# A retention and low-rank mixer kernel: batch 0's q loaded one head at a time, and a planner that counts on more loads in flight

## The chip, the core and the metric

The kernel runs on one core of one Trainium2 chip. A core has five engines that run side by side: TensorE (PE in the profile; matrix products, with weight loads shown as PEld), VectorE (DVE), ScalarE (ACT), GpSimd (POOL) and SyncE (SP, which here only issues DMAs). Each follows its own list of instructions in order, and waits for the others through semaphores. Sixteen DMA engines move data between the memory (HBM) and the on-chip memory SBUF. Products go into PSUM, which has eight banks.

The metric is the time of one execution on the device, in microseconds (us). Less is better.

## The reference

Inputs are q, k and v of shape (4 batches, 8 heads, 768 steps, 64), a pair of low-rank matrices U (768 x 32) and V (32 x 768), and the weights of two layers, w_ch1 (512 x 2048) and w_ch2 (2048 x 512), all float32. First comes a retention (an attention with a decay for each head):

```
gamma = 1 - 2 ** (-5 - arange(H)); scale = 1 / sqrt(D)
for t in range(S):
    state = gamma * state + outer(k[:, :, t], v[:, :, t])
    y[:, :, t] = scale * (q[:, :, t] @ state)
```

The heads are laid side by side to x (4, 768, 512), and then

```
h = x.transpose(0, 2, 1) @ U @ V
u = x + h.transpose(0, 2, 1)
out = u + maximum(u @ w_ch1, 0) @ w_ch2
```

## The kernel before

**Stages.** The four batches go through the same stages: load q, k and v; scale and cast them to bf16; transpose k and q; scores, masked by time order; states that carry earlier blocks; a mix that gives x; the low-rank product (`proj`, `expand`, in batch 0 `low0` and `high0`) that gives u; a transpose of u (tile uT); the first layer ("up" products M<-w1b,uT, with a relu into gT) and the second (products of gT, or of its sums S, with w2b or its sums T). The second layer uses a scheme that trades eight products of blocks for seven and some sums on VectorE and GpSimd (tiles S and T). While TensorE does one batch's layers, the next batch's attention is put between them. Batches 0 and 1 go by pairs of heads (`pair`, c = 0 to 3); batches 2 and 3 by blocks of 128 steps (`chunk`).

**Loads.** The profile gives all plain loads of q, k, v, U and V the line L342, since they go through one helper, `load`. In batch 0 the list `ORDER` says "k0 q0 q1 k1 v0 k2 q2 q3 k3 v1 v2 v3": each name is one load of a tensor's head pair, 384 KB, into one of nine buffers `in`. `load_pair` makes them. k0 and v3 come in two loads of one head each, the others in one load. A q load has 256 rows of 1536 bytes (128 partitions times two heads), a k or v load has 768 rows of 512 bytes. All loads of batch 0 write a common key "in", and so keep their order in SP's list. The loads of batch 1 and 2 onward are made by `load_pair` and `loads_chunk` (three loads of 1024 rows for each block). Weights come by GpSimd's own queue (`load_cast`, L357), which casts to bf16 on the way. In batch 1 the transposes of k (kT<-kb, L542) and in batches 2 and 3 those of k and q (L717) and of u (uT<-x, L841) are DMAs too, issued by SP in the same queue as the loads.

**Casts.** In `pair`, the casts of q are two, one for each head (`cast`, qb<-in, L299 on GpSimd or L297 on ScalarE). The planner may give either to either engine in batch 0. The transposes of q (six TensorE instructions of L309) wait for both; ScalarE then copies the result (qT<-M).

**The planner.** The order of the work isn't written out. Every piece of work is a step with a cost on each engine that could do it, a due time `at`, an earliest time `hold`, and what it reads and writes. `Plan.run` runs a model of the core at build time: at each turn it takes the step that could start first, and among equals the one with the earlier due time. The sequence so found, with the engine chosen for each step, is the program. The planner's times are not in the program; only the order, and the choice of engines, are. For steps of SP (loads and DMA transposes) the model has two limits, in `when`: at most 8 DMAs of SP in flight, and at most 2350 rows (`op.dma[0]`) in flight together; a step that would go over is modelled as starting later, and another may then go first.

**Dummies.** Up to a planned 27 us, `fill` puts products of zeros (M<-gT, 128x512) into TensorE's planned gaps, so that it stays active. Their number follows from the planned gaps.

Of the kernel before, what the change touches and what calls it, by code (L numbers as in the profile page):

```python
# [65 lines left out]
class Plan:  # L66
# [11 lines left out]
    def add(s, cost, fn, rd=(), wr=(), at=0.0, mode=None, lock="", dma=None,  # L78
            hold=0.0, slack=0.0):
        op = Step(len(s.steps), cost, fn, at, mode, lock, dma, hold, slack)  # L80
        op.rd, op.wr = list(rd), list(wr)
        before = set()
        for r in rd:
            if r in s.writer:
                before.add(s.writer[r])
        for w in wr:
            before.update(s.readers.get(w, ()))
            if w in s.writer:
                before.add(s.writer[w])
        for r in rd:  # L90
            s.readers.setdefault(r, []).append(op)
        for w in wr:
            s.writer[w] = op
            s.readers[w] = []
        before.discard(op)
        for p in before:
            p.after.append(op)
        op.left = len(before)
        s.steps.append(op)
        return op  # L100
# [16 lines left out]
    def run(s, fill=None, until=0.0, traced=None, behind=None):  # L117
        free = {e: 2.03 if e == "A" else 0.85 for e in s.OVER}
        lock = {"D": 0.0, "P": 0.0}
        todo = {e: [] for e in s.OVER}  # L120
        mode, queues, flying, order = None, Queues(), [], []

        def offer(op):
            for e in op.cost:
                todo[e].append(op)

        def when(op, e):
            t = max(free["P" if e == "Q" else e], op.ready(e))
            if e in op.lock:
                t = max(t, lock["D" if e == "P" else "P"])  # L130
            if e == "S":
                fly = sorted((o.end, o.dma[0]) for o in flying if o.end > t)
                if len(fly) >= 8:
                    t = max(t, fly[-8][0])
                while fly and sum(n for _, n in fly) + op.dma[0] > 2350:
                    t = max(t, fly.pop(0)[0] - 1.2)
            return t

        for op in s.steps:
            if not op.left:  # L140
                offer(op)
        while len(order) < len(s.steps):
            best = None
            for e, ops in todo.items():
                for op in ops:
                    t = when(op, e)
                    turn = op.mode and op.mode[0] != mode
                    key = (t, op.at + (0.3 if turn else 0.0), op.n)
                    if best is None or key < best[0]:
                        best = (key, e, op)  # L150
            (t0, _, _), e, op = best
            for e2 in op.cost:
                todo[e2].remove(op)
            order.append(op)
            d = op.cost[e]
            op.start, op.eng = t0, e
            if op.dma:
                nd, lead = op.dma[0], op.dma[2]
                if e == "S":
                    flying = [o for o in flying if o.end > t0] + [op]  # L160
                free["P" if e == "Q" else e] = op.free = t0 + d
                queues.put(e, t0 + d + lead, op)
            else:
                if e == "PE":
                    if mode is not None and op.mode[0] != mode:
                        d += s.SWITCH
                    mode = op.mode[1]
                free[e] = op.free = t0 + d - s.OVER[e]
                op.end = t0 + d
                if e in op.lock:  # L170
                    lock[e] = op.end
            for n in op.after:
                n.pre.append(op)
                n.left -= 1
                if not n.left:
                    offer(n)
        order.sort(key=lambda o: (o.start, o.n))
        last, sums = 0.0, None
        used = s.spans(order, BANKS)
        for op in order:  # L180
            if op.eng == "PE":
                gap = op.start - last - 0.12
                if fill and op.start < until and gap > 0.1:
                    free = [(max([b for _, b in used[k] if b <= last + 0.25] + [0.0]), k)
                            for k in BANKS if not any(
                                a < op.start + 1e-6 and b > last + 0.25
                                for a, b in used[k])]
                    if free:
                        fill(gap, op.start, min(free)[1])
                last = op.free  # L190
            at = len(traced()) if traced else 0
            op.fn(op.eng)
            if traced and op.eng in op.lock:
                new = [i for i in traced()[at:]]
                if op.eng == "D":
                    sums = (new[-1], op.end)
                elif sums and op.start - sums[1] < 3.0:
                    behind(new[0], sums[0])
# [3 lines left out]
def kernel(  # L202
# [12 lines left out]
    P = 128  # L215
# [113 lines left out]
    def behind(late, early):  # L329
        tc.add_manual_dep(late, early.name, mybir.DependencyInfo(  # L330
            mybir.DependencyClass.Sync, mybir.DependencyReason.DATA),
            reason="order")
# [3 lines left out]
    def load(dst, src, nd, size, wr, at, hold=0.0, rd=(), late=0.0, air=0):  # L336

        n = len(flights)
        flights.append(None)

        def f(e):
            nc.sync.dma_start(out=dst, in_=src)  # L342
            flights[n] = nc.cur_bb.bb.instructions[-1]
            if air and n >= air:
                behind(flights[n], flights[n - air])
        add({"S": 0.43 + 0.00014 * nd}, f,
            [*rd, ("air", n - air)] if air else rd, [*wr, ("air", n)], at,
            dma=(nd, 0.009 + size / 27200, 0.8, 1.26 + late), hold=hold)
# [83 lines left out]
    for c in range(NC):  # L432
# [3 lines left out]
            at=-5 + c, lock="DP")  # L436
# [3 lines left out]
        at=26.0, hold=26.0)  # L440
# [11 lines left out]
    def gate(t, key, src, rd, at):  # L452

        add({"P": 0.18}, lambda e: nc.gpsimd.tensor_copy(out=t[:1, :1], in_=src), [rd],
            [(key, z) for z in range(2)], at)

    def lag(nm, c):
        n = ORDER.index(nm + str(c))
        return 1.6 if n == 11 else min(0.2 * n, 0.7) if n else -0.7

    def load_pair(nm, b, c, at, hold=0.0, after=None, halves=False):


        t, key = new_in()
        gets[nm, b, c] = (t, key)
        if after:
            gate(t, key, *after, at - 0.1)
        src = {"k": k, "q": q, "v": v}[nm][b, ds(2 * c, 2)]
        first = [] if b else ["in"]
        if nm == "q":  # L470
            load(t.rearrange("p (i x) -> p i x", i=2),
                 src.rearrange("i (p j) d -> p i (j d)", p=P), 256, 1536,
                 [(key, i) for i in range(2)] + first, at, hold, late=2.0 if b else lag(nm, c))
            return
        for g in ([(0,), (1,)] if halves else [(0, 1)]):
            n = NB * len(g)
            load(t[:, ds(384 * g[0], 128 * n)].rearrange("p (n x) -> p n x", n=n),
                 src[ds(g[0], len(g))].rearrange(
                     "i (n p j) d -> p (i n) (j d)", p=P, j=2),
                 P * n, 512, [(key, i) for i in g] + first, at + 0.01 * g[0], hold,  # L480
                 late=(2.0 if b else lag(nm, c)) + (0.7 if g[0] and nm + str(c) == ORDER[-1] else 0.0),
                 air=0 if b else AIR)
# [579 lines left out]
    land, t = {}, 1.85  # L1062
# [4 lines left out]
    def early(*names):  # L1067
        for n in names:
            load_pair(n[0], 0, int(n[1]), -10 + land[n], halves=n in ("k0", ORDER[-1]))
# [87 lines left out]
    for i, (lo, n) in enumerate(W1):  # L1157
# [3 lines left out]
                  late=(1.2, 1.9, 1.9, 2.6, 2.6)[i], air=3 if i == 4 else 0)  # L1161
# [4 lines left out]
    for j in range(4):  # L1166
# [3 lines left out]
                  hold=WH[4] + 2.4 * (j + 1),  # L1170
                  late=(2.6, 2.9, 3.3, 4.6)[j], air=3)
    gates = [(w2b[:1, 4 * j, :1], ("w2", j)) for j in (1, 2, 3)]
    for c in range(3):
        for z, nm in enumerate("kqv"):
            load_pair(nm, 1, c, T[0] + 16 + 4 * c + 0.1 * z,
                      after=gates[c])
# [15 lines left out]
    first = mlp(0, T[0], SPAN, banks=["RR0", "RR1", "M1", "M2", "Y", "M0"])  # L1192
# [5 lines left out]
    for c in ALLC:  # L1198
        at = T[0] + 16 + 6 * c
# [67 lines left out]
```

## Time and profile before

| | us |
|---|---|
| three runs | 218.96, 219.72, 220.25 |
| their median | 219.72 |
| the profiled execution | 220.99 |
| its span, first to last instruction | 219.2 |
| TensorE busy in it | 210.3 (96%) |
| mean granted clock of TensorE | 0.984 |

In the profile, the slices divide the span into 40 equal parts of 5.5 us and give the busy share of each engine in tenths; PEclk is the clock that TensorE was granted, in tenths of the full one. The chain is followed back from the last instruction: at each step to whatever released it, or to the instruction before it on its engine; "issue" is time in which the engine waited for nothing that the profile shows. A row of the order of time gives the start, the duration, the engine (a q behind it stands for its sequencer, which issues DMAs), the line, the operation, what is written and read, and in brackets how long the engine was idle before and what ended that. In a table by stretches each engine's column is its busy time with the number of its instructions; then follow the granted clock, the busy share of the DMA engines and the rate in GB/s.

### The profile page before, as it was taken

To read this page: it belongs to the slowest core of one execution; us is meant where nothing else is said; L and a number is where in the kernel's file an instruction comes from. 1 tells how busy PE (TensorE), PEld (TensorE's weight loads), DVE (VectorE), ACT (ScalarE), POOL (GpSimd) and SP (SyncE) were. 2 spreads that over 40 slices of the span, in tenths; PEclk is the share of its full clock that TensorE was granted. 3 is DMA by queue.
4 is the path that set the end of the run, shared out by engine and by line. 5 is a ranking of instruction groups with operands and counts; after the bars stand their busy time and mean duration, and the time that the engine had idled before them with its cause. 6 is when DMAs were issued, how large, how long until landed. Compare 5 with 4: busy or idle time off the path is not lost.

```text
span 219.2 us, 5787 instructions
## 1 busy us (share of the span) xinstructions
PE 210.3 (96%) x2377; PEld 152.1 (69%) x2377; DVE 138.0 (63%) x250; ACT 102.6 (47%) x194; POOL 86.2 (39%) x140
## 2 busy tenths in 40 slices
PE   7787999999999999999999999999999999999993
PEld 2465744478888885457888875568888854588882
DVE  6287534999996645799479745739298614235532
ACT  3585336579663334676732017677320047661000
POOL 3637123117539654143356543334614510003330
PEclk9997699999999999999999999999999999999999
DMA  5999999996999979999897669789503940000222
GB/s 163 324 312 215 191 205 200 232 303 138 199 214 274 231 150 177 221 166 184 144 208 200 147 171 256 152 185 166 109 0 110 194 131 3 0 0 3 96 97 96
DMA packets 84266, 35.99 MB, mean 164 GB/s; under 512 B 63120, under 2 KB 82320, under 8 KB 84240
## 3 DMA queue, kind: packets, MB, share of 16 engines
q1 hardware_dynamic: 78048, 26.72, 58.3%
q0 software_dynamic: 6192, 8.91, 18.9%
q8 instruction: 18, 0.29, 0.6%
q14 instruction: 8, 0.07, 0.1%
HBM read 27.75 MB, written 6.29 MB: 155 GB/s over the span
## 4 chain that ended last, share of the span: by engine, by line
PE 87%; DMA 6%; SPq 3%; issue 1%; DVE 1%; ACT 0%; POOL 0%; DVEq 0%
PE M L305 72%; PE RR L305 10%; PE Y L305 4%; SPq L342 3%; DMA in<-in_k_dram 3%; DMA kT<-kb 3%; PE RR L309 1%; POOL kb L302 0%; DVE o L992 0%; DVE kb L302 0%; PE Y L309 0%; ACT x L297 0%; ACT s L297 0%; DVEq L992 0%
## 5 line engine op out<-in xcount | busy, mean ns | idle before, releaser
L305 PE MATMUL M<-uT,w1b 128*128 128x256 bf16 (+1 forms) x500 | 86.3, 325 | 0.0
L305 PEld LDWEIGHTS <-w1b 128*128 128x128 bf16 x512 | 48.4, 98 | 29.9 <-issue 0.4
L881 ACT ACTIVATE gT<-M 128x512 bf16<-128x512 f32 x83 | 49.3, 597 | 35.0 <-PE M L305 34.5
L305 PEld LDWEIGHTS <-gT 128*128 128x128 bf16 x405 | 39.0, 99 | 8.9 <-issue 2.6
L302 POOL TENSOR_TENSOR t<-s,x 128x256 f32<-128x256 f32 x36 | 23.2, 672 | 39.2 <-ACT s L297 34.5
L305 PEld LDWEIGHTS <-S 128*128 128x128 bf16 (+1 forms) x336 | 28.6, 100 | 4.2 <-issue 0.2
L305 PE MATMUL M<-w2b,S 128*128 128x256 bf16 x192 | 26.7, 273 | 0.0
L305 PE MATMUL M<-w2b,gT 128*128 128x256 bf16 x192 | 26.5, 273 | 0.1
L305 PE MATMUL M<-T,gT 128*128 128x256 bf16 x192 | 24.9, 273 | 0.0
L992 DVE TENSOR_TENSOR r<-M,t 128x256 f32<-128x256 f32 x24 | 10.1, 422 | 21.6 <-POOL t L302 20.4
L302 POOL TENSOR_TENSOR qb<-in,gqn 128x512 bf16<-128x512 f32 x12 | 12.5, 1042 | 22.7 <-DMA in<-in_q_dram 10.9
L302 DVE TENSOR_TENSOR S<-gT 128x1024 bf16<-128x1024 bf16 x12 | 8.6, 716 | 16.0 <-ACT gT L881 15.3
L297 ACT ACTIVATE s<-M 128x256 f32<-128x256 f32 x12 | 4.6, 384 | 27.4 <-PE M L305 27.3
L1036 POOL DMA_DIRECT2D out_dram<-o x18 | 10.1, 561 | 16.4 <-DVE o L992 16.3
L812 DVE TENSOR_TENSOR x<-RR,x 128x512 bf16<-128x512 f32 x24 | 15.5, 682 | 1.1 <-PE RR L305 1.1
L732 DVE TENSOR_TENSOR a<-RR,mask 128x1024 bf16<-128x1024 f32 x12 | 14.1, 1218 | 1.6 <-PE RR L305 1.5
L302 POOL TENSOR_TENSOR vb<-in,gkn 128x512 bf16<-128x512 f32 x12 | 12.5, 1046 | 6.3 <-DMA in<-in_v_dram 4.7
L593 DVE TENSOR_TENSOR a<-RR,mask 128x1024 bf16<-128x1024 f32 (+1 forms) x12 | 11.1, 949 | 4.9 <-PE RR L305 4.8
L992 DVE TENSOR_TENSOR o<-M,r 128x256 f32<-128x256 f32 x24 | 10.1, 419 | 4.5 <-PE M L305 4.2
L305 PE MATMUL M<-T,S 128*128 128x256 bf16 x96 | 12.6, 273 | 0.0
L297 ACT ACTIVATE kb<-in 128x384 bf16<-128x384 f32 (+1 forms) x16 | 8.8, 574 | 5.5 <-DMA in<-in_k_dram 5.3
L305 PE MATMUL RR<-qT,kT 64*64 64x128 bf16 (+1 forms) x288 | 8.9, 223 | 2.2 <-issue 1.4
(100 smaller groups left out, 246.6 us busy)
## 6 DMA issues: line engine op xcount, KB each, us to landing
out_dram<-o POOLq DMA_DIRECT2D x18, 256.0 KB, 3.7
in<-in_q_dram SPq DMA_DIRECT2D x8, 384.0 KB, 6.2
in<-in_k_dram SPq DMA_DIRECT2D x12, 256.0 KB, 4.5
in<-in_q_dram SPq DMA_DIRECT2D x12, 256.0 KB, 4.5
in<-in_v_dram SPq DMA_DIRECT2D x12, 256.0 KB, 4.9
in<-in_k_dram SPq DMA_DIRECT2D x7, 384.0 KB, 7.1
in<-in_v_dram SPq DMA_DIRECT2D x7, 384.0 KB, 6.9
w2b<-in_moe_w_ch_dram POOLq DMA_DIRECT2D x4, 512.0 KB, 7.4
```

The source lines that it names most:

```text
L297: nc.scalar.activation(dst, src, AF.Copy)
L302: (nc.vector if e == "D" else nc.gpsimd).tensor_tensor(dst, a, b, op=op)
L305: nc.tensor.matmul(out_, lhsT, rhs, start=start, stop=stop, skip_group_check=True)
L309: nc.tensor.transpose(out_, in_, ident)
L342: nc.sync.dma_start(out=dst, in_=src)
L593: lambda e, bs=bs, lo=lo, w=w: nc.vector.tensor_tensor(av[:, :, ds(bs[0], len(bs))], RR[lo // 2][:, :, :w].rearrange("p i (b t) -> p i b t ...
L732: add({"D": cD(2 * DM)}, lambda e: nc.vector.tensor_tensor(a[:, :2 * DM].rearrange("p (n t) -> p n t", t=P), RR[z].rearrange("p i (n t) -> ...
L812: add({"D": cD(512)}, lambda e, xj=xj, src=src: nc.vector.tensor_tensor(xj, src, xj, op=ALU.add), [f"RR{c}" for c in cc] + kk, kk + [("u", ...
L881: nc.scalar.activation(dst, src, AF.Relu)
L992: add({"D": cD(HD)}, lambda e: nc.vector.tensor_tensor(dst, bankof(bank)[:, :HD], src, op=op), [bank] + rd, wr, at - 2)
L1036: lambda e: (nc.sync if last else nc.gpsimd).dma_start(out=dst, in_=src), rd, [("out", b, at)], at,
```

## The change

Two things change. In batch 0, each q load of two heads becomes two loads, one for each head, 128 rows of 1536 bytes and 192 KB each. The second has a due time later by 0.01. Each writes only the key of its own head's half of the buffer, so that each cast waits for its own load. Other batches keep one load for both heads. And the planner's limit of rows in flight goes from 2350 to 3300, for all steps of SP in all batches.

```diff
             if e == "S":
                 fly = sorted((o.end, o.dma[0]) for o in flying if o.end > t)
                 if len(fly) >= 8:
                     t = max(t, fly[-8][0])
-                while fly and sum(n for _, n in fly) + op.dma[0] > 2350:
+                while fly and sum(n for _, n in fly) + op.dma[0] > 3300:
                     t = max(t, fly.pop(0)[0] - 1.2)
...
         if nm == "q":
-            load(t.rearrange("p (i x) -> p i x", i=2),
-                 src.rearrange("i (p j) d -> p i (j d)", p=P), 256, 1536,
-                 [(key, i) for i in range(2)] + first, at, hold, late=2.0 if b else lag(nm, c))
+            for g in ([(0,), (1,)] if b == 0 else [(0, 1)]):
+                n = len(g)
+                load(t[:, ds(384 * g[0], 384 * n)].rearrange("p (i x) -> p i x", i=n),
+                     src[ds(g[0], n)].rearrange("i (p j) d -> p i (j d)", p=P),
+                     P * n, 1536, [(key, i) for i in g] + first, at + 0.01 * g[0],
+                     hold, late=2.0 if b else lag(nm, c))
             return
```

## The prediction

> **What bounds the kernel now.** I read the page first: the busy shares, the slices and the shares of the chain that ended last.
>
> ```profile
> span 219.2 us, 5787 instructions
> PE 210.3 (96%) x2377; PEld 152.1 (69%) x2377; DVE 138.0 (63%) x250; ACT 102.6 (47%) x194; POOL 86.2 (39%) x140
> PE   7787999999999999999999999999999999999993
> PEclk9997699999999999999999999999999999999999
> DMA  5999999996999979999897669789503940000222
> PE 87%; DMA 6%; SPq 3%; issue 1%; DVE 1%; ACT 0%; POOL 0%; DVEq 0%
> ```
>
> TensorE is full from the fifth slice (a slice is 5.5 us) to the last but one. Before that neither it nor its clock is full, while the DMA engines are. So there are two regimes: a start of some 26 us in which loads set the pace, and then one engine that never rests. Next the busy time by stretch, cut at the edges of the clock's drop.
>
> ```profile
> core 0: us, PE busy (x) PEld busy (x) DVE busy (x) ACT busy (x) POOL busy (x), PEclk, DMA share, GB/s
> 5.79:12.62 6.83, 5.38 (x100) 3.29 (x98) 2.86 (x5) 4.63 (x8) 3.53 (x6) 1.00 1.12 330
> 12.62:19.45 6.83, 4.84 (x112) 3.54 (x111) 5.38 (x8) 5.55 (x10) 4.75 (x8) 1.00 1.16 266
> 19.45:26.27 6.82, 6.53 (x123) 5.00 (x124) 4.08 (x7) 2.34 (x5) 2.19 (x4) 0.50 1.22 190
> 26.27:33.10 6.83, 6.83 (x77) 3.75 (x76) 2.74 (x7) 2.42 (x6) 1.48 (x2) 1.00 1.24 205
> 33.10:60.00 26.90, 26.90 (x279) 18.27 (x277) 22.83 (x37) 18.53 (x37) 10.12 (x22) 1.00 1.04 214
> 60.00:100.00 40.00, 39.90 (x557) 27.54 (x556) 29.13 (x51) 20.71 (x41) 20.43 (x27) 1.00 1.04 207
> ```
>
> From 26.27 TensorE is idle 0.1 us in 74. Nothing can be won there without taking work from it; something can be lost. Between 19.45 and 26.27 it ran at half its clock while 96% busy: that is where time lies. The chain of waits, in order of time, shows what came just before.
>
> ```profile
> 8.40 6.65 DMA in<-in_k_dram
> 15.05 0.02 issue
> 15.07 0.57 DVE kb L302
> 15.71 0.84 POOL kb L302
> 18.10 0.27 PE RR L305 x12
> 18.37 1.36 issue
> 19.74 0.53 PE RR L305 x12
> ```
>
> The chain goes through the last k load of batch 0 (issued 8.40, landed 15.05), its two scalings, and the scores of the last head pair, which stop halfway: twelve matmuls, 1.36 us with no releaser that the profile knows, twelve more. No q load is on it.
>
> **The change, part by part.** *More issues.* Four q loads of batch 0 become eight. SP's issues in order of time (start, us), and from the list of DMAs the KB and the us to landing of the two half-size k loads:
>
> ```profile
> 0.74 0.98 SPq L342 DMA_DIRECT2D in<-in_k_dram  x2
> 1.77 0.99 SPq L342 DMA_DIRECT2D in<-in_q_dram  x2
> 5.62 2.73 SPq L342 DMA_DIRECT2D in<-in_q_dram  x2
> in<-in_k_dram SPq DMA_DIRECT2D x2, 192.0 KB, 2.7
> ```
>
> The k loads of the first row are already one head each, 192 KB, and cost SP the same half microsecond as a q load of two heads: an issue is paid per DMA. So SP gets 4 x 0.5 = 2.0 us more. The third row says that SP has this time: two issues that need 0.99 took 2.73, as SP stood 1.7 us before a full queue. Queued behind the new issues are the k load of the chain above and the v loads. That k load took 6.65 us to land where one with nothing ahead took 2.7 (half its size), so it lay some 4 us in the queue, against 2.0 us. I take 0. Without that cover it would be the 2.0 us.
>
> *The same bytes in eight pieces.* Rows stay 1536 bytes and the number of them stays; what is added is four completions. The stretches above moved 330 GB/s with whole loads queued back to back. I take 0; the ends are 0 and the same 2.0 us, if each new load left a hole as long as its issue.
>
> The Trainium skill, "DMA: Bandwidth & Descriptors", under "Anatomy of one DMA" and "Bandwidth", speaks against this part: a DMA costs about 2.0 us fixed plus its bytes at 436 GB/s, and loads should be batched to 1 MiB. By it, as an estimate, one head's load is 2.45 us and two heads' 2.90, so four splits would add 8.0 us if loads ran one at a time. The rows show them overlapping: the 2.7 us of a 192 KB load agrees with the page's figure for one load, but two such loads were issued within 0.98 us.
>
> *Earlier first halves.* Each head's cast now waits for its own half.
>
> ```profile
> 6.22 0.81 ACT L297 ACTIVATE kT<-Y 128x768 bf16<-128x768 bf16 x1 [2.75 <-PE Y L309]
> 6.51 0.50 POOL L299 CAST qb<-in 128x384 bf16<-128x384 f32 x1 [3.89 <-DMA in<-in_q_dram]
> 6.92 0.51 ACT L297 ACTIVATE qb<-in 128x384 bf16<-128x384 f32 x1
> 7.58 0.50 PE L309 MATMUL M<-ident,qb 128*128 128x128 bf16 x6 [0.76 <-ACT qb L297]
> ```
>
> The transposes need both halves, and the second lands when the whole load did. What counts is the later cast: it stood on ScalarE behind kT until 6.92, while GpSimd could begin at 6.51. At best the pair of casts ends 0.41 us sooner. What is late next is k (landed 15.05), so of that gain nothing reaches the end: 0, with 0.4 us as the bound on the good side.
>
> *The order of batch 0.* All its loads write one common key, so SP's order stays. The planner may hand a cast to the other engine, and may put other dummy matmuls into TensorE's gaps. I take 0; its ends are rivals A and C, since the clock's drop and the stall lie just behind this work.
>
> *The limit of 3300.* This number makes nothing wait on the chip; it decides what the planner puts where in SP's program. In batch 1 a k, a q and a v load count 768, 256 and 768 rows, together 1792. The next k (2560) was too much for 2350 and the next q (2048) was not:
>
> ```profile
> 38.37 0.39 SPq L342 DMA_DIRECT2D in<-in_k_dram  x1
> 38.86 0.50 SPq L342 DMA_DIRECT2D in<-in_q_dram  x1
> 39.46 1.10 SPq L342 DMA_DIRECT2D in<-in_v_dram  x1
> 41.20 0.57 SPq L342 DMA_DIRECT2D in<-in_q_dram  x1
> 41.82 1.81 SPq L342 DMA_DIRECT2D in<-in_k_dram  x1
> 49.98 1.31 SPq L542 DMA_TRANSPOSE kT<-kb  x1
> ```
>
> With 3300 that k fits beside the three (2560, and 2816 with the q), so k comes before q, and about one more load of 768 rows gets in ahead of the transpose that follows; in batches 2 and 3 it is three loads of 1024 rows where it was two. The queue is in order, so a kT transpose then lands one load later. A load is 384 KB (393 thousand bytes); at the 214 GB/s of 33.10:60.00 that is 1.84 us. Who waits for a transpose, by the chain (first two rows), SP's issues, the kT transposes' times to landing, and TensorE in order of time:
>
> ```profile
> 54.12 6.33 DMA kT<-kb
> 60.50 0.53 PE RR L305 x24
> 65.42 1.99 SPq L542 DMA_TRANSPOSE kT<-kb  x1
> DMA to landing us min/median/max: 3.0/5.3/6.4
> 73.37 0.25 PE L305 MATMUL RR<-qT,kT 64*64 64x128 bf16 x2
> ```
>
> The second pair's kT landed at 60.45 and was used at once. While batch 0's products are left, a late kT only makes the planner put more of those first. They are used up when batch 1's own first layer must start, and that hangs on the last pair. Its kT was issued at 65.42, landed within 6.4 us, so by 71.82, and was used at 73.37: 1.55 us of slack. One load more makes it 1.84 - 1.55 = 0.3 us late. Ends: 0 (the extra load was on its way earlier anyway) and two loads, 3.68 - 1.55 = 2.1 us. A gain is excluded there, since TensorE has no idle time to give back. I take 0.3, one load being what the limit admits. For batches 2 and 3 I take 0, as TensorE idles 0.1 us of 60:100 and their loads come a whole batch ahead; the same 2.1 us bounds it.
>
> Sum: 0 + 0 + 0 + 0 + 0.3 = +0.3 us. The profiled execution took 220.99 us, its span of 219.2 and 1.8 around it, so it would be 221.3; it lies 1.27 us over the median of the runs, 219.72, and against that median the forecast is 220.0.
>
> **The rivals.** *A, the stall and the halved clock go (faster).* The clock was halved at the edge of a stretch of 6.83 us in which TensorE was busy 4.84 (71%); the stretch before, with 5.38 (79%), kept it. So the bound lies between, and half a microsecond of work moved across 12.62, or the 1.36 us stall falling elsewhere, would decide it. For it: q's work can come up to 0.4 us earlier, and dummies can move. Against it: moving q's work to before 12.62 empties the stretch that already failed. Price: at least the stall, 1.36 us; at most that and half of the 6.53 busy microseconds, 4.6. The loads still arriving then take part of it, so I put the middle of the lower half, 2.2: 217.5 us.
>
> On this the Trainium skill, "TensorE: Matmul & The Clock Gate", under "Why this matters for your kernels", names a gap of over about 3 us as what drops the clock. The trace differs: its longest gap in the failed stretch is 1.36 us. Its "Part 4: PE-mode transpose" holds that transposes do not count as busy in the same way, which no row here separates; by that, earlier q transposes would change nothing in the clock.
>
> *B, transposes behind two more loads (slower).* The last pair's kT 3.7 us later, decided when the delay passes the 1.55 us of slack: +2.1, so 221.8 us. For it: that a single kT already took 6.33 us to land. Against it: the planner knows the queue is in order, and the DMA engines move the same bytes.
>
> *C, the clock drops one stretch earlier (slower).* If work or dummies leave 5.79:12.62 so that its 5.38 falls towards 4.84, the next stretch runs at half speed: 4.84 us more of work against 6.83 - 4.84 = 1.99 us of idle time, +2.85: 222.6 us. Against it: its 330 GB/s and its work barely change.
>
> *D, smaller loads are slower (the page's rule).* The rows give at most the 2.0 us worked out for SP's issues, and the time 221.7. The queue was full, so I give it little. By the skill's own figures ("DMA: Bandwidth & Descriptors", above) it would be up to 227.7.
>
> *E, the change does nothing.* q was not on the chain and the transposes keep their slack: 219.7. I count it with the forecast, from which it differs by 0.3 us.
>
> **How the numbers follow.** Runs of one kernel spread over 218.96 to 220.25, so 0.5% (1.1 us) is about what a measurement can tell from no change. Chances: forecast with E 0.36, A 0.28, B 0.24, C 0.08, D 0.04. A is faster, B, C and D are slower: faster 0.28, same 0.36, slower 0.36. The predicted time is 220.0; its own range is 218.6 to 220.8. The 8 in 10 range goes down to 217.4, which holds A's price and leaves out its larger half to 4.6 us (about 0.1), and up to 222.2, which holds B and D and leaves out C (about 0.1).
>
> **What would show it.** SP: eight q issues of about 0.5 us before 9 us, and the k load of the chain landing at 15.0 still. GpSimd's first q cast before 6.5 and the transposes of q at 7.2 to 7.6. The stall of about 1.4 us near 18.4 and a half clock for one stretch again. In batch 1, k before q at the fourth load, and kT landing up to 1.8 us later, with idle time of TensorE before batch 1's first layer of some tenths. The prediction is wrong if the half clock is gone or doubled, if TensorE idles over 1 us between 26 and 215, or if the k load lands after 16.

## The result and the profile after

The changed kernel is slower: a median of 222.7 us over six runs (221.44 to 225.26) against 219.57 over six of the kernel before; ratio 1.0141, 95% interval 1.0096 to 1.0187, so a loss of 1 to 2%. My range ended at 222.2, and its forecast was 220.0. The profiled execution took 223.79 us with a span of 222.0. (Ratios here and below compare undisturbed runs alone, so a median of all runs can stand a little apart from them.)

The page of the changed kernel: span, busy shares, slices, chain.

```profile
span 222.0 us, 5795 instructions
PE 210.4 (95%) x2377; PEld 151.4 (68%) x2377; DVE 137.6 (62%) x250; ACT 103.6 (47%) x197; POOL 85.9 (39%) x137
PE   7879999998999999699999999989999999999993
PEclk9979999999999999999999999999999999999999
DMA  6899999999999999995927979997004630000222
PE 56%; DMA 17%; POOL 9%; SPq 5%; DVE 4%; issue 3%; ACT 3%; POOLq 0%; ACTq 0%; DVEq 0%
```

TensorE has the same number of instructions and the same busy time, 210.4 for 210.3 us. What is new are holes: a 6 in the seventeenth slice and an 8 in the tenth and the twenty-seventh, where there were only nines, and a chain of which DMA now has 17% and TensorE 56%. By stretches, the changed kernel first and then the one before:

```profile
core 0: us, PE busy (x) PEld busy (x) DVE busy (x) ACT busy (x) POOL busy (x), PEclk, DMA share, GB/s
26.30:60.00 33.70, 32.96 (x342) 20.93 (x334) 24.75 (x43) 21.29 (x42) 13.54 (x25) 1.00 1.21 237
60.00:100.00 40.00, 38.00 (x517) 26.36 (x515) 26.69 (x48) 18.87 (x38) 21.33 (x28) 1.00 1.27 214
100.00:160.00 60.00, 59.16 (x639) 44.62 (x638) 40.52 (x60) 30.29 (x59) 25.71 (x31) 1.00 0.84 157
```

```profile
26.30:60.00 33.70, 33.70 (x354) 21.99 (x353) 25.53 (x44) 20.95 (x42) 11.60 (x24) 1.00 1.08 212
100.00:160.00 60.00, 60.00 (x635) 46.28 (x634) 38.95 (x62) 28.77 (x54) 28.79 (x36) 1.00 0.87 170
```

With the 39.90 of 40.00 that the kernel before has in the middle stretch, TensorE idled 0.1 us in these 133.7; now it idles 0.74 + 2.00 + 0.84 = 3.6 us. The waits of TensorE from 26 us on name most of it (total, times, longest):

```profile
PE M L305 <- ACT gT L884: 2.6, 2, 1.8
PE RR L305 <- DMA kT<-kb: 0.7, 1, 0.7
```

The two big ones wait for ScalarE's relu (gT). The chain of waits through both, in order of time:

```profile
85.97 6.20 DMA in<-in_k_dram
92.23 0.63 ACT kb L297
92.86 0.50 ACT gT L884
93.40 1.45 PE M L305 x6
...
139.50 4.75 DMA in<-in_k_dram
144.34 0.63 ACT kb L297
144.97 0.50 ACT gT L884
145.50 1.46 PE M L305 x6
```

This is the pattern of the whole case. A k load of the next batch was issued at 85.97 and landed 6.2 us later. In ScalarE's list its cast stands ahead of a relu of the present batch. ScalarE is in order, so the relu, whose own input was ready, waited for the load; the bank that the relu would have emptied was not free, and TensorE stopped for 1.8 us. ScalarE's waits for k loads in sum, in the changed kernel and then in the kernel before:

```profile
ACT kb L297 <- DMA in<-in_k_dram: 17.1, 7, 5.0
```

```profile
ACT kb L297 <- DMA in<-in_k_dram: 5.3, 5, 2.6
```

What the limit did to the plan shows in the same block of the kernel before. Its cast of k is on ScalarE too, but later in the list, at 96.75 where it is now at 92.23, and it waits for nothing:

```profile
96.75 0.63 ACT L297 ACTIVATE kb<-in 128x512 bf16<-128x512 f32 x1
```

In two later profiles, both at the full clock, the same cast stands at 95.37 in the old order (the split in the old order) and at 90.70 in the changed kernel, after 1.1 and 3.0 us of waiting; only in the second does TensorE stop behind a relu.

Against the loss stands a gain at the start: the same products stood at 36.24 in the profile of before and stand at 35.10 here.

```profile
36.24 2.27 PE M L305 x10
```

```profile
35.10 2.27 PE M L305 x10
```

It is not the change's; it differs by the execution, for the most part with the clock. In the first 26 us this was halved for 6.8 us in the profile of before and for 3.45 us in this one. Where it was not halved there, these products start at 33.6 (the split in the old order), 33.7 (the changed kernel once more) and 35.3 (the limit in batch 1 alone); with the limit at 5000, where it was halved again, at 36.0.

For the same reason the 0.1 us of idle time before the change is too good a measure. The split in the old order has the plan of the kernel before, and its profile has the full clock:

```profile
33.10:60.00 26.90, 26.74 (x319) 18.84 (x316) 24.25 (x40) 18.40 (x37) 11.57 (x22) 1.00 1.19 243
60.00:100.00 40.00, 40.00 (x533) 27.82 (x531) 28.66 (x48) 19.97 (x39) 20.93 (x27) 1.00 1.12 195
100.00:160.00 60.00, 58.38 (x612) 44.90 (x611) 37.30 (x62) 27.20 (x52) 27.81 (x35) 1.00 0.85 166
```

There TensorE idled 0.16 + 0 + 1.62 = 1.8 us without the limit, and in the kernel before with two casts moved, also at the full clock, 2.4 us. In the second profile of the changed kernel it idled 3.8 us between 26.3 and 160. Like for like, 1.4 to 2.0 us of holes are new. That the later start of the profiled kernel before hid its holes is argued, not shown. ScalarE's wait for k loads was 8.4 us with the split in the old order and 17.3 us in the second profile of the changed kernel.

### The profile page after: what moved, and what is told of

The parts are those of the page before. It is cut to its first block, busy times and chain, and to the rows that moved or that the text cites. A ratio compares the mean times of both kernels' runs of the same rounds, so it can differ in the third digit from the quotient of the medians.

```text
span 222.0 us, 5795 instructions
## 1 busy us (share of the span) xinstructions
PE 210.4 (95%) x2377; PEld 151.4 (68%) x2377; DVE 137.6 (62%) x250; ACT 103.6 (47%) x197; POOL 85.9 (39%) x137
## 4 chain that ended last, share of the span: by engine, by line
PE 56%; DMA 17%; POOL 9%; SPq 5%; DVE 4%; issue 3%; ACT 3%; POOLq 0%; ACTq 0%; DVEq 0%
PE M L305 48%; DMA in<-in_k_dram 8%; PE RR L305 6%; DMA in<-in_q_dram 5%; SPq L342 3%; POOL vb L302 3%; DMA kT<-kb 3%; POOL t L302 3%; POOL qb L302 2%; PE Y L305 2%; SPq L720 2%; DVE S L302 1%; POOL out_dram L1039 1%; DMA T<-in_moe_V_dram 1%; ACT kb L297 1%
## 5 line engine op out<-in xcount | busy, mean ns | idle before, releaser
L884 ACT ACTIVATE gT<-M 128x512 bf16<-128x512 f32 x83 | 48.7, 596 | 31.5 <-PE M L305 31.1
L305 PEld LDWEIGHTS <-S 128*128 128x128 bf16 (+1 forms) x336 | 28.1, 97 | 3.9
L302 POOL TENSOR_TENSOR vb<-in,gkn 128x512 bf16<-128x512 f32 x12 | 13.1, 1090 | 14.7 <-DMA in<-in_v_dram 7.6
L302 DVE TENSOR_TENSOR S<-gT 128x1024 bf16<-128x1024 bf16 x12 | 9.3, 776 | 14.1 <-ACT gT L884 13.8
L302 POOL TENSOR_TENSOR qb<-in,gqn 128x512 bf16<-128x512 f32 x12 | 13.1, 1093 | 11.6 <-DMA in<-in_q_dram 9.2
L297 ACT ACTIVATE kb<-in 128x512 bf16<-128x512 f32 (+1 forms) x17 | 9.3, 577 | 17.1 <-DMA in<-in_k_dram 17.1
L305 PEld LDWEIGHTS <-kb 64*64 64x64 bf16 (+2 forms) x200 | 7.9, 106 | 3.3 <-issue 0.6
```

Of the source, the lines that this page charges most:

```text
L297: nc.scalar.activation(dst, src, AF.Copy)
L302: (nc.vector if e == "D" else nc.gpsimd).tensor_tensor(dst, a, b, op=op)
L305: nc.tensor.matmul(out_, lhsT, rhs, start=start, stop=stop, skip_group_check=True)
L884: nc.scalar.activation(dst, src, AF.Relu)
```

## The experiments

Theory 1: the limit costs the time, through the order that the planner makes with it (casts of k ahead of relus). Theory 2: the split costs it, through slower loads.

**The split alone.**

```diff
-                while fly and sum(n for _, n in fly) + op.dma[0] > 3300:
+                while fly and sum(n for _, n in fly) + op.dma[0] > 2350:
```

> The changed kernel with the limit of rows in flight put back to 2350: eight q loads in batch 0, the order of batches 1 to 3 planned as before. Theory 1 (the limit's order costs the time: k loads of batches 2 and 3 arrive after the place that the plan gave their casts, ScalarE stands before them, relus come late and TensorE stops): no such stop, TensorE idle under 0.5 us between 26 and 215, and since the start of the changed kernel was some 1.1 us earlier than before, 218.0 to 219.5 us. Theory 2 (the split costs it: the eight smaller loads move slower, 262 against 330 GB/s in 5.79:12.62, and everything after is late): 221.5 to 223 us.

Measured: ratio 0.9987 (0.9948 to 1.0026). Theory 1's side, though without a gain. Its profile, the longest of its ten executions (222.76 us), shows no stop behind the relu. But TensorE was not idle under 0.5 us, as expected: it waited 1.5 us for a kT, 1.1 us for a cast of q and 0.6 us for scaled v.

**The limit alone**, in the kernel before.

```diff
-                while fly and sum(n for _, n in fly) + op.dma[0] > 2350:
+                while fly and sum(n for _, n in fly) + op.dma[0] > 3300:
```

> The kernel before with the limit at 3300 and nothing else: four q loads in batch 0, and the order of batches 1 to 3 that the higher limit plans. Theory 1: the stops of TensorE (3.6 us in sum in the changed kernel) are there, the 1.1 us that its start won are not: 222 to 224 us. Theory 2: 219 to 220.5 us, with no stop over 0.5 us.

Measured: ratio 1.0089 (1.0045 to 1.0133), with both stops behind the relu. TensorE's waits:

```profile
PE M L305 <- ACT gT L881: 3.1, 2, 2.2
```

So the limit costs time without any split.

**The split in the old order.**

```diff
-            nc.sync.dma_start(out=dst, in_=src)
+            for d_, s_ in heads or [(dst, src)]:
+                nc.sync.dma_start(out=d_, in_=s_)
...
```

(`heads` holds the two single-head loads for a q of batch 0.)

> The kernel before with its planned order untouched on all engines; each step that loads q in batch 0 issues two DMAs of one head in place of one of two. This is the split on the chip alone, without what the planner makes of it. Theory 1: within 0.5% of before (218.5 to 220.7), and as its order of batch 0 is that of before, no gain of the start either. Theory 2: 221.5 us or more, with the second k load landing near 10.6 as in the changed kernel and not near 8.9.

Measured: ratio 1.0006 (0.9955 to 1.0057). Eight loads of 192 KB in place of four of 384 KB cost nothing that can be measured; Theory 2 falls by the time. The sign named for it does not decide: the second k load landed near 9.8, between 8.9 and 10.6.

**The limit by batch**, in the kernel before: 3300 for the planner's time under 59 us (batch 1's loads), then from 59 us on (batches 2 and 3).

```diff
-                while fly and sum(n for _, n in fly) + op.dma[0] > 2350:
+                while fly and sum(n for _, n in fly) + op.dma[0] > (3300 if t < 59 else 2350):
```

> The kernel before with the limit of 3300 only where the planner's time is under 59 us, so for batch 1's loads and first transposes, and 2350 from there. My prediction put the cost here (transposes of k behind one load more): ratio 1.002 or more with TensorE waiting for kT. Theory 1: the cost is in batches 2 and 3, so ratio 0.995 to 1.004.

> The kernel before with the limit of 3300 only where the planner's time is 59 us or more, so for the loads of batches 2 and 3 and what SP issues beside them. Theory 1: the stops behind ScalarE's relu are there, and nearly all of the limit's cost: ratio 1.006 to 1.013. If batch 1 bears it: 0.996 to 1.004.

Measured: batch 1 alone 0.9997 (0.9952 to 1.0042), batches 2 and 3 alone 1.0072 (1.003 to 1.0114). TensorE's waits, in the first and in the second:

```profile
PE RR L305 <- DMA kT<-kb: 1.1, 1, 1.1
```

```profile
PE Y L305 <- DVE ns L299: 1.0, 1, 1.0
PE RR L305 <- DMA kT<-kb: 0.8, 1, 0.8
PE M L305 <- ACT gT L881: 0.7, 1, 0.7
```

A wait for kT in batch 1 is there, though not at the pair that I had named, and does not show in the time; the cost lies in batches 2 and 3. In the second profile the wait behind the relu is only one of three: the stops differ with the order.

**Telling the planner that the loads come late**, in the changed kernel and, as control, in the kernel before.

```diff
-                 [(key, z) for z in range(2)], at, hold)
+                 [(key, z) for z in range(2)], at, hold, late=4.0)
```

> The changed kernel, with the planner told that the loads of batches 2 and 3 land 4 us later than its model says (the tables of both kernels show SP's issues in these batches several us behind the place that the plan has for them). Queue, limit and split stay. Theory 1a (the cost is that ScalarE's casts of k are put ahead of relus in the belief that k is there): the 1.8 and 0.8 us stops of TensorE behind ScalarE's relu go, ScalarE's wait for k loads falls from 17 us to under 8, ratio 0.99 to 1.004. Theory 1b (the deeper queue itself brings the data too late, whatever the plan believes): TensorE stops elsewhere, ratio still 1.008 or more.

> The kernel before, with the same 4 us of lateness told to the planner: the control for the run on the changed kernel. TensorE did not stop in batches 2 and 3 before, so nothing is to be won: ratio 0.995 to 1.005 by both theories. Clearly below 0.995 would mean that the lateness is a gain by itself.

Measured: 1.0959 (1.0888 to 1.103) and 1.1843 (1.1745 to 1.1941). In the changed kernel ScalarE's wait for k loads fell to 0.2 us and no stop behind the relu is left, as theory 1a had it. But both ratios are far off, and the experiment does not tell the theories apart: the lateness enters the landing times that the limit counts by, so a load stays "in flight" 4 us longer in the model and the next ones are held back. The attention of batches 2 and 3 then comes too late: TensorE waited 9.7 us for transposes of u in the first, and 10.4 us for those of q and 9.0 us for those of u in the second. That the control lost more fits its lower limit, which holds more back, but no run separates this. The two settings belong together: how many rows may be in flight has a meaning only together with when the planner believes that they land.

**Only the two casts moved**, in the changed kernel's own order: after the plan is made, the fifth block's cast of k in batches 2 and 3 goes from ScalarE to GpSimd, at the same place.

```diff
...
+        for op in order:
+            op.eng = op.move or op.eng
...
         cast(kd[:, :DM], kin[:, :DM], DM, zz(kk), zz(kdk), at - 6, eng="PA")
+        if n == 4:
+            plan.steps[-1].move = "P"
```

> The changed kernel with its order untouched, but the two casts of k behind which ScalarE's relu stood as TensorE stopped 1.8 us (near 91.6) and 0.84 us (near 144.7), the fifth block's of batches 2 and 3, run on GpSimd at the same place in the order. No load, no limit and no other step is changed. Theory 1a: both stops go, 2.6 us, so the ratio falls from 1.014 to 1.000 to 1.006. Theory 1b (the data itself is late for TensorE's next need): TensorE stops for a transpose instead, at the same place, and the ratio stays over 1.008.

Measured: 0.9977, but from 0.9898 to 1.0057, as it rests on three of ten executions; the median of all ten, 223.19 us, is above the 221.70 of the kernel before beside it. Both stops were gone from its profile. Since that interval is wide and no changed kernel ran beside it, this version was run again beside the changed kernel and a control (the same two casts moved in the kernel before).

> The changed kernel as it is, beside the next two on one chip: it gives the measure for them. Both theories: ratio 1.010 to 1.018.

> Once more the changed kernel with the two casts of k on GpSimd at their place, as the first timing left an interval from 0.99 to 1.006. Theory 1a: ratio 0.997 to 1.005, and clearly under that of the changed kernel beside it. Theory 1b: not distinct from the changed kernel's.

> The control: the same two casts put on GpSimd in the order of the kernel before, which did not stop there. Theory 1a: 0.997 to 1.003, nothing to win. If it is under 0.995, the move is a gain by itself and says nothing of the change.

Measured on one chip: changed kernel 1.0161 (1.0117 to 1.0205), with the casts moved 1.0061 (1.0019 to 1.0103), control 1.0008 (0.9971 to 1.0044). The expectation's 0.997 to 1.005 was missed narrowly, but the casts take 1.0 of the 1.6 points away ((1.0161 - 1.0061) x 220.31 us of before on that chip = 2.2 us), and gain nothing in the kernel before. The direction is clear by these intervals, the size is not. Among the executions with a mean granted clock of 0.998 or more, the changed kernel has a mean of 222.80 us (three) and the version with the casts moved 221.28 us (six), 1.5 us apart; the medians of all executions, 223.08 and 222.37 us, are 0.7 us apart. TensorE's waits in the changed kernel of this set:

```profile
PE M L305 <- ACT gT L884: 3.0, 2, 1.8
PE RR L305 <- DMA kT<-kb: 0.7, 1, 0.7
```

and with the casts moved, with the moved cast itself from the order of time:

```profile
PE RR L307 <- DMA kT<-kb: 3.4, 2, 2.3
91.44 0.89 POOL L301 CAST kb<-in 128x512 bf16<-128x512 f32 x1
```

The stops behind the relu are gone. In this profile a stop of 2.3 us for kT came up instead, which the profile of the first run of the same kernel has at 0.5 us:

```profile
PE RR L307 <- DMA kT<-kb: 0.8, 2, 0.5
```

So with ScalarE out of the way the late data still bites at times, at its next user, which is what theory 1b named. The span of this profile is 220.8 us, against 221.0 of the changed kernel beside it and 219.1 of the first run with the casts moved. The late transposes may be the other 0.6 points; that is argued from one profile in two, not shown.

**Other depths**, in the changed kernel: a limit at which two loads of 1024 rows and a transpose fit but a third load doesn't, and one at which four fit.

```diff
-                while fly and sum(n for _, n in fly) + op.dma[0] > 3300:
+                while fly and sum(n for _, n in fly) + op.dma[0] > 3000:
```

> The changed kernel with a limit of 3000: beside two loads of 1024 rows a transpose of 512 is let in (2560), a third load (3072) is not. If the third load is the cause: ratio as of the split alone, 0.995 to 1.003, ScalarE's wait for k loads under 13 us. If letting transposes in is: as the changed kernel, 1.009 or more.

```diff
-                while fly and sum(n for _, n in fly) + op.dma[0] > 3300:
+                while fly and sum(n for _, n in fly) + op.dma[0] > 5000:
```

> The changed kernel with a limit of 5000, so that four loads of 1024 rows are let in. If each load more makes the plan put the casts earlier against the real landings, the cost grows: ratio 1.018 or more and a longer wait of ScalarE for k loads than 17 us. If the buffers or the eight DMAs in flight already set the order at 3300: as the changed kernel, 1.010 to 1.018.

Measured: 1.0024 (0.9976 to 1.0072) at 3000 and 1.025 (1.0172 to 1.0327) at 5000. With 1.0141 and 1.0161 at 3300, and 0.9987 at 2350, the cost comes with the third load (3072 rows). Whether it grows with the fourth is not settled: the intervals at 3300 and 5000 overlap, and all four executions at 5000 had a mean granted clock of 0.984 to 0.992. ScalarE's wait for k at 3000, and TensorE's waits at 5000:

```profile
ACT kb L297 <- DMA in<-in_k_dram: 14.5, 9, 5.1
```

```profile
PE RR L305 <- DMA kT<-kb: 3.3, 2, 2.0
PE RR L305 <- DMA qT<-qb: 1.7, 1, 1.7
```

The first row corrects me: 14.5 us of waiting, where I had expected under 13, and no cost that can be measured; no stop behind the relu is in that profile. At 5000 I was wrong the other way: ScalarE waited 6.6 us for k, where I had expected more than 17, and the time was longer all the same, with TensorE waiting for the transposes directly. So how long ScalarE waits is no measure of the cost. What fits the profiles is whether TensorE needs what stands behind the wait.

No version beat the kernel before clearly; the split alone, at 0.9987, is the same as before.

## Why the prediction was wrong

*More issues, and the same bytes in eight pieces: 0.* Right, by 1.0006 and 0.9987 with the split alone. The first half of q was cast early, and in this profile the pair's transposes began at 7.82, not earlier than 7.58 before:

```profile
5.38 0.50 POOL L299 CAST qb<-in 128x384 bf16<-128x384 f32 x1 [2.75 <-DMA in<-in_q_dram]
5.38 4.45 SPq L342 DMA_DIRECT2D in<-in_q_dram  x1
7.16 0.92 ACT L297 ACTIVATE qb<-in 128x384 bf16<-128x384 f32 x2
7.82 0.49 PE L309 MATMUL M<-ident,qb 128*128 128x128 bf16 x6 [0.35 <-ACT qb L297]
```

The reason is the one given: the second cast stands on ScalarE behind kT. In the second profile of the changed kernel the transposes began at 6.90, so this start differs by the run. In the profile shown SP stood 4.45 us at one q issue, so my sign "eight issues before 9 us" failed, and the last k load was issued at 11.30 and its scaling began at 17.2, past my sign of 16. In the second profile that scaling began at 15.6. Neither run of the split alone shows a cost in time. Rival D is out by the same runs. The Trainium skill gives its fixed 2.0 us for each DMA ("DMA: Bandwidth & Descriptors", "Anatomy of one DMA") as a fit to DMAs that GpSimd issues. For these loads, which SP issues and which overlap, four more of them added nothing measurable (1.0006).

*The order of batch 0: 0, and rivals A and C.* The stretch of 6.8 us at half clock comes and goes with the execution. In the profile of the changed kernel the clock was halved for 3.45 us:

```profile
13.90:17.35 3.45, 3.33 (x53) 2.39 (x44) 2.06 (x4) 2.91 (x6) 1.01 (x2) 0.51 1.03 298
```

In its second profile, in the one of the two casts moved in the kernel before, and in others, it was not halved in the first 26 us at all; with the limit at 5000 it was, in 19.45:26.30 (0.51), as in the kernel before. Of 85 later executions of the kernel before, 61 had a mean clock of 0.996 or more, the others down to 0.974. So A's gain was there to be had in either kernel, by the run, and so was C's loss: in the profile of the changed kernel 5.79:12.62 fell to 4.64 us of work and the drop came earlier, as C had it. The bound that I read between 71% and 79% of busy time does not hold. With the limit alone that stretch had 4.01 us of work (59%), in the second profile of the changed kernel 4.26 us (62%), and no drop followed in either. I had built two rivals and their prices on what one execution showed.

*The limit in batch 1: +0.3.* The order came as said, k ahead of q at the fourth load, and a wait for kT with it (0.7 us):

```profile
39.58 0.39 SPq L342 DMA_DIRECT2D in<-in_k_dram  x1
40.06 0.49 SPq L342 DMA_DIRECT2D in<-in_q_dram  x1
40.66 0.54 SPq L342 DMA_DIRECT2D in<-in_v_dram  x1
42.17 0.70 SPq L342 DMA_DIRECT2D in<-in_k_dram  x1
42.96 2.95 SPq L342 DMA_DIRECT2D in<-in_q_dram  x1
48.71 1.64 SPq L545 DMA_TRANSPOSE kT<-kb  x1
```

But the wait is at the first pair's kT, not at the last's, on which the term rests. The transposes did not come one load later either: the last pair's kT was issued at 62.64 where it had been 65.42, and its products ran at 73.31, as before (73.37). In time the limit in batch 1 measured 0.9997 with an interval of half a percent to each side, so a cost of 0.3 us is neither confirmed nor refuted; the way to it was wrong.

*The limit in batches 2 and 3: 0.* This is the step that failed. The reason I gave was that TensorE idles 0.1 us of 60:100 "and their loads come a whole batch ahead". They don't, at the third load in flight: it landed 6.2 us after its issue, with ScalarE already waiting. I had asked who waits for the transposes, and not who waits for the loads, nor what is queued behind the cast that does. ScalarE is busy 47% of the time, but its list is in order and holds the relus that TensorE lives on. Alone, in the kernel before, this term measured 1.6 us (0.0072 x 221.59 us; 0.7 to 2.5 by the interval), where I had 0 with a bound of 2.1. The whole change measured 3.1 us (222.7 - 219.57). Of the changed kernel's loss, the two casts are between 0.7 and 2.2 us, by which executions are compared; the rest is open.

*Rival B* had the right sign and the right setting, the limit, but the wrong place: batch 1's transposes in place of ScalarE's casts in batches 2 and 3. That its 221.8 us is nearer to the result than the forecast is luck.

Open: the limit alone measured 1.0089, and with the split 1.0141 and 1.0161. The intervals overlap, so whether the two parts together cost more than the limit does is not settled.

## What to carry to other kernels

A planner's model of how much may be in flight is part of the schedule, not a safety margin: raising it here put a cast of k 4.5 us earlier in ScalarE's list (92.23 for 96.75), ahead of its data, and a consumer that waits takes with it whatever stands behind it, here the relus on which the full engine depends. When a change lets loads go deeper, look in the profile for each engine that has both a wait for a load and work that the bound engine needs, however idle that engine is. And check a feature of one profiled execution, such as a stretch at a lower clock, against a second one, before a price or a comparison is built on it.

## What the runs showed of the hardware

A stop of TensorE can cost more than itself. In the profile of the limit alone, the 2.25 us stop was followed by half the clock; stretches of that profile:

```profile
82.50:89.27 6.77, 6.77 (x52) 3.14 (x50) 3.47 (x7) 3.99 (x8) 3.07 (x4) 1.00 1.24 226
89.27:92.78 3.51, 1.26 (x7) 0.48 (x5) 0.56 (x2) 2.29 (x5) 1.04 (x1) 1.00 0.98 154
92.78:96.20 3.42, 3.42 (x23) 1.65 (x23) 3.39 (x5) 1.00 (x2) 0.00 (x0) 0.50 0.86 173
96.20:100.00 3.80, 3.80 (x41) 2.25 (x40) 2.25 (x4) 3.12 (x6) 2.04 (x2) 1.00 0.92 156
```

TensorE was busy 1.26 of 3.51 us (36%), with no single gap over 2.25 us, and then ran 3.42 us at 0.50. The Trainium skill, "TensorE: Matmul & The Clock Gate", under "Why this matters for your kernels", puts the danger at gaps of over about 3 us; a shorter one was followed by it here. The 1.8 us stops of the changed kernel were not, and neither was the 2.3 us stop with the casts moved, in which TensorE was busy 0.24 of 2.57 us. So the length of a stop alone does not decide it.
